# A staged kernel of attention and two expert layers: decode pieces of half the size, and one weight's loads issued earlier

## The chip, the cores and the metric

One core of a Trainium2 chip runs the whole program. The metric is the device time of one execution in microseconds; three runs of the kernel before gave 1173.73, 1179.30 and 1179.88, median 1179.3.

## The reference, cut to what matters

```python
def _attn_ref(q, k, v):                       # batch 4, 8 heads, 1152 positions, 64 wide
    q_pool = q.reshape(B, H, S // 2, 2, D).mean(axis=3)
    attn = softmax(scale * q_pool @ k.T)      # 576 queries against 1152 keys
    return attn @ v

def _moe_ref(x, w_in, w_out):                 # 2304 x 512 -> 2048 -> 512
    h = x @ w_in
    g = np.where(h >= 1, h, np.where(h <= -1, 0.0, (h + 1) ** 2 / 4))
    return g @ w_out
# then 8 experts of 512 -> 1024 -> 512, one for each token
```

The first layer's weights, `w_in` and `w_out`, come as 64-bit floats, so they are read as pairs of 32-bit words and turned into float32 by integer operations.

## The kernel before, in words

Three stages follow each other: attention, the first layer (`Moe1`), the routed experts (`Moe2`). The program's order is written out by hand: each engine runs its instructions in the order of the source.

*Attention* works on 16 pairs of heads, 9 query tiles of 128 each: 144 steps `s` (`t = s % 9`, and 8 more steps that only finish). In a step TensorE writes the scores of one tile into PSUM (L232), VectorE reads them into `e` and takes the minimum (L236), TensorE transposes the exponentials of an earlier tile (L261), ScalarE and VectorE split these into a high and a low part (L270, L272), and TensorE does eight matmuls of the product with `v` (L286). There is one PSUM buffer for scores, so the scores of step s + 1 wait for L236 of step s. GpSimd prepares the next pair, in the order of the steps: sum and split of q (L165, L57, L168, L169), split of k (L57, L174) and of v (L57, L195). SP issues nearly all DMAs.

At the end of each step `aside(s)` is called. From step 72 on it brings in the first three weights (`EARLY = 3`), 18 steps each: `ws.load(j)` issues two DMAs of 512 KB (a 128-wide slice of `w_in`, one of `w_out`), and `ws.decode(j)` gives six pieces for VectorE, three for each half: mask and shift (L458), a mask and or (L462), a shift and or (L466). After each third piece GpSimd copies the high part (L57) and subtracts (L451). The loads of weight 3 are issued at step 146 (`last` is 135).

`stage` is a pool of two large tiles (tag `m`) and two small ones (tag `w`); loads, decoded words and, at the end of attention, the rows of x for group 0 take turns in it. `tail()` at step 135 issues the DMAs of those rows; from step 139 on one x item a step is multiplied on GpSimd (L549, L550) and split by ScalarE and VectorE (L553, L554).

*Moe1* runs 16 steps of 128 hidden columns for each of four groups of tokens. `h_mm` writes h into one of two PSUM buffers (L577); `h_act` computes the activation: ScalarE (L592, L595), VectorE's product (L596), ScalarE's copy (L598), and the low part on GpSimd (L600). `fill()` puts one more decode piece into VectorE's queue, ahead of L596 and behind it; in group 0 five pieces a step decode weights 3 to 15, and the load of each half of the next weight follows the third and the sixth piece.

Of the kernel before, what the change touches and what calls it, by code (L numbers as in the profile page):

```python
# [8 lines left out]
F32 = mybir.dt.float32  # L9
F32R = mybir.dt.float32r  # L10
BF16 = mybir.dt.bfloat16
U32 = mybir.dt.uint32
I32 = mybir.dt.int32
AF = mybir.ActivationFunctionType
ALU = mybir.AluOpType
# [31 lines left out]
EARLY = 3  # L47
# [7 lines left out]
def hi_part(e, out, in_, nc):  # L55
    if e is nc.gpsimd:
        e.tensor_scalar(out=out, in0=in_, scalar1=1.0, scalar2=1.0, op0=ALU.mult, op1=ALU.mult)  # L57
    elif e is nc.scalar:
        e.copy(out, in_)
    else:  # L60
        e.tensor_copy(out, in_)
# [336 lines left out]
class Weights:  # L398
# [41 lines left out]
    def decode(self, j):  # L440


        nc = self.nc
        raw = self.raw
        hi, lo = (self.pools(j).tile([128, 2, 512], F32R, name=f"w{c}{j}", tag=f"w{c}{j}") for c in "hl")
        self.t[j] = hi, lo
        out = []

        def split(i, w, e):
            hi_part(e, hi[:, i], w, nc)  # L450
            nc.gpsimd.tensor_sub(out=lo[:, i], in0=w, in1=hi[:, i].bitcast(F32))  # L451

        for i in range(2):
            box = {}

            def first(i=i, box=box):
                box["w"] = self.stage.tile([128, 512], U32, name="wf", tag="w")
                nc.vector.tensor_scalar(out=box["w"], in0=raw[j, i][:, :, 1], scalar1=0x07FFFFFF, scalar2=3,  # L458
                                        op0=ALU.bitwise_and, op1=ALU.logical_shift_left)

            def second(i=i, box=box):
                nc.vector.scalar_tensor_tensor(out=box["w"], in0=raw[j, i][:, :, 1], scalar=0xC0000000,  # L462
                                               in1=box["w"], op0=ALU.bitwise_and, op1=ALU.bitwise_or)

            def third(i=i, box=box):
                nc.vector.scalar_tensor_tensor(out=box["w"], in0=raw[j, i][:, :, 0], scalar=29, in1=box["w"],  # L466
                                               op0=ALU.logical_shift_right, op1=ALU.bitwise_or)
                if j < EARLY:
                    split(i, box["w"].bitcast(F32), nc.gpsimd)
                else:  # L470
                    self.late.append(lambda: split(i, box["w"].bitcast(F32), nc.scalar))

            out += [first, second, third]
        return out
# [651 lines left out]
class Moe2:  # L1126
# [57 lines left out]
    def split(self, which, i):  # L1184
        k, h = divmod(i, 2)
        r, hi, lo = (self.w[which + c, k][:, h] for c in "rhl")
        self.nc.scalar.copy(hi, r)  # L1187
        self.nc.vector.tensor_sub(out=lo, in0=r, in1=hi.bitcast(F32))  # L1188
# [212 lines left out]
def tile_kernel(tc, q, k, v, w_in, w_out, emb, tau, w1, w2, out):  # L1401
    nc = tc.nc
    with ExitStack() as ctx:
        def pool(name, bufs, **kw):
            return ctx.enter_context(tc.tile_pool(name=name, bufs=bufs, **kw))

        one = pool("one", 1)
        dram = pool("dram", 1, space=DRAM)
        wa = pool("w_a", 1)
        stage = pool("stage", 2)  # L1410
        ctx.enter_context(tc.manual_schedule())

        idf = one.tile([128, 128], F32, name="idf")
        half = one.tile([128, 1], F32, name="half")
        zero = one.tile([128, 64], F32, name="zero")
        eps = one.tile([128, 1], F32, name="eps")
        cn = dict(idf=idf, half=half, zero=zero, eps=eps)
        xs = Scratch(dram)

        late = {}  # L1420
        ws = Weights(nc, w_in, w_out, stage, lambda j: wa if j < EARLY else late["w"])
        m1 = Moe1(tc, xs, ws, cn)
        with ExitStack() as actx:
            at = Attention(tc, q, k, v, xs, cn)
            make_identity(nc, idf)
            nc.vector.memset(half, 0.5)
            nc.vector.memset(eps, 1e-9)
            nc.vector.memset(zero, 0.0)
            at.open(actx)
            for w in range(2):  # L1430
                nc.scalar.copy(at.qts[0][:, w, NQ:NQ + 64], zero)
            for h in range(2):
                at.load_qk(0, h)
            rt = Router(tc, one, dram, emb, tau, cn)
            last = (at.NPAIR - 1) * 9
            pieces = []

            def aside(s):
                if s == 12:
                    late["consts"] = rt.consts(stage)  # L1440
                if 12 <= s < 12 + 3 * 6 and s % 3 == 0:
                    next(late["consts"], None)
                if s == 28:
                    late["emb"] = rt.experts(stage)
                if s in (31, 34):
                    late["emb"][(s - 31) // 3]()
                j, c = divmod(s - (last - 63), 18)
                if 0 <= j < EARLY:
                    if c == 0:
                        ws.load(j)  # L1450
                    elif c == 2:
                        pieces.extend(ws.decode(j))
                if pieces and s % 3 == 0:
                    pieces.pop(0)()
                if s == last + 11:
                    ws.load(EARLY)

            def tail():
                late["x0"] = tc.alloc_tile_pool(name="x0", bufs=1, side="right", reuse_waits="tile")
                m1.x_alloc(0, late["x0"])  # L1460

                for i in range(5):
                    m1.x_raw(0, i)
                    m1.x_load(0, i, ws.rows(i, 5))
                evs = {}

                def one(i):
                    evs[i] = m1.x_item(0, i)
                return [[lambda i=i: one(i) if i < 5 else None, lambda i=i: evs[i - 1]() if i else None]
                        for i in range(6)]  # L1470

            at.run(aside, tail)
        late["w"] = pool("w_b", 1, reuse_waits="tile")

        def weight(i, dt):
            j, c = divmod(i, 2)
            return ws.pools(j).tile([128, 2, 512], dt, name=f"e{i}", tag="w" + "hl"[c] + str(j))

        def xpool():
            late["x0"].release()  # L1480
            late["d_x"] = tc.alloc_tile_pool(name="d_x", bufs=1, side="right", reuse_waits="tile")
            return late["d_x"]

        rt.rtp, rt.rsm = pool("b_rt", 2, reuse_waits="tile"), pool("b_rs", 2, reuse_waits="tile")
        m2 = Moe2(tc, rt, w1, w2, out, weight, xpool, cn)
        with ExitStack() as bctx:
            x1 = bctx.enter_context(tc.tile_pool(name="x1", bufs=1, reuse_waits="tile"))
            m1.open(bctx)
            items = m1.run(rt, [late["x0"], x1], m2)
        with ExitStack() as dctx:  # L1490
            m2.open(dctx)
            m2.run(items)
        late["d_x"].release()
# [39 lines left out]
```

## Time and profile before

| what | us |
|---|---|
| median of three runs | 1179.3 |
| the profiled execution | 1178.18 |
| its span, first to last instruction | 1176.4 |
| TensorE matmul busy | 1135.4 (97%) |
| VectorE busy | 883.1 (75%) |
| ScalarE busy | 753.2 (64%) |
| GpSimd busy | 580.7 (49%) |

Attention takes the first 483 us of the span. A timeline row gives an instruction's start and length in us, engine, line, operation and operands, and in brackets the idle time of its engine just before it and what ended that. PE is TensorE, DVE VectorE, ACT ScalarE, POOL GpSimd, SPq the queue of SP. Ends of matmuls are modelled.

### The profile page before, as it was taken

The page shows a single profiled execution, that of the slowest core. Times are in us where ns is not written, and L with a number is a line of the kernel's source. Part 1 is how long each engine was busy: PE and PEld are TensorE (multiplying, and loading weights), DVE is VectorE, ACT ScalarE, POOL GpSimd, SP SyncE. Part 2 cuts the span into 40 slices and gives each one's busy share as a digit, 9 for nine tenths or more (in the row PEclk, how much of TensorE's full clock was granted, in tenths as well). Part 3 has the DMA queues.
Part 4 walks back from the last instruction along what each step waited for, and adds up shares of the span by engine and source line. Part 5 has one row for each costly group of instructions (what it writes and reads, how often), then busy time and mean ns, then how long its engine had stood idle before and what let it go on. Part 6 is the DMA issues. An engine that isn't in the chain of part 4 may idle for free. (4 is left out here: it accounts for less than half of the span.)

```text
span 1176.4 us, 21181 instructions
## 1 busy us (share of the span) xinstructions
PE 1135.4 (97%) x7315; PEld 1056.2 (90%) x7315; DVE 883.1 (75%) x1593; ACT 753.2 (64%) x1477; POOL 580.7 (49%) x499
## 2 busy tenths in 40 slices
PE   7999999999999999799999999999999999999997
PEld 6999999999999999799789999998889899887886
DVE  6898898899999998698866664764355776676765
ACT  5888888887878787555554445544435566566764
POOL 6998988887888885267762121112010221121212
PEclk9999999999999999899999999999999999999999
DMA  7777777786868758354532222120222121286443
GB/s 181 175 186 180 175 168 175 172 212 134 207 163 204 168 139 177 101 170 152 161 113 67 59 69 73 41 68 20 90 82 100 45 64 38 80 271 208 158 140 122
DMA packets 87877, 156.14 MB, mean 133 GB/s; under 512 B 26535, under 2 KB 44967, under 8 KB 87744
## 3 DMA queue, kind: packets, MB, share of 16 engines
q1 hardware_dynamic: 83040, 142.34, 45.4%
q0 software_dynamic: 4336, 11.58, 3.0%
q8 instruction: 67, 1.10, 0.4%
q10 hardware_dynamic: 368, 0.59, 0.2%
q14 instruction: 66, 0.54, 0.2%
HBM read 145.84 MB, written 20.08 MB: 141 GB/s over the span
## 5 line engine op out<-in xcount | busy, mean ns | idle before, releaser
L236 DVE TENSOR_SCALAR_CACHE_REDUCE e<-sc 128x1152 f32<-128x1152 f32 x144 | 194.7, 1352 | 24.3 <-PE sc L232 23.0
L243 ACT ACTIVATE e<-e,nm 128x1152 f32<-128x1152 f32 x144 | 183.6, 1275 | 9.0 <-DVE e L236 8.9
L232 PE MATMUL sc<-kT,qt 128*128 128x384 f32 x780 | 160.1, 340 | 11.7 <-DVE e L236 9.6
L270 ACT CAST pth<-pa 128x768 fp32r<-128x768 f32 (+2 forms) x160 | 116.3, 737 | 78.6 <-PE pa L261 78.4
L272 DVE TENSOR_TENSOR ptl<-pa,pth 128x768 fp32r<-128x768 f32 (+2 forms) x160 | 138.8, 876 | 17.7 <-ACT pth L270 5.5
L1188 DVE TENSOR_TENSOR e<-e,e 128x512 fp32r<-128x512 f32 x200 | 129.5, 688 | 28.3 <-ACT e L1187 12.3
L232 PEld LDWEIGHTS sc<-kT,qt 128*128 128x128 f32 x780 | 132.8, 189 | 14.5 <-DVE e L236 11.7
L596 DVE SCALAR_TENSOR_TENSOR u<-h,u 128x320 f32<-128x320 f32 (+1 forms) x112 | 55.7, 497 | 107.8 <-ACT u L595 107.4
L592 ACT ACTIVATE u<-h,half 128x320 f32<-128x320 f32 (+1 forms) x112 | 59.7, 533 | 109.5 <-PE h L577 109.3
L1284 PE MATMUL d_po<-e,e 128*128 128x512 f32 x504 | 121.0, 393 | 0.6 <-DVE e L1188 0.6
L261 PE MATMUL pa<-idf,e 128*128 128x128 f32 x864 | 117.6, 272 | 3.0 <-DVE ptl L272 3.0
L1187 ACT CAST e<-e 128x512 fp32r<-128x512 f32 x200 | 113.7, 619 | 0.6 <-issue 0.3
L609 PE MATMUL y<-wh,gh 128*128 128x512 f32 x288 | 113.9, 395 | 0.0
L609 PE MATMUL y<-wh,gl 128*128 128x512 f32 x288 | 113.7, 395 | 0.0
L609 PE MATMUL y<-wl,gh 128*128 128x512 f32 x288 | 113.6, 394 | 0.0
L261 PEld LDWEIGHTS pa<-idf,e 128*128 128x128 f32 x864 | 102.9, 140 | 8.3 <-issue 2.2
L1284 PEld LDWEIGHTS d_po<-e,e 128*128 128x128 f32 x504 | 92.6, 188 | 19.2 <-DVE e L1188 1.0
L1292 POOL DMA_INDIRECT out<-d_ob,d_rec x19 | 22.5, 1186 | 176.0 <-ACT d_ob L1291 119.3
L598 ACT CAST gh<-u 128x320 fp32r<-128x320 f32 (+1 forms) x112 | 52.3, 467 | 79.9 <-DVE u L596 79.9
L286 PE MATMUL av<-pth,vh 128*128 128x288 f32 x576 | 103.1, 306 | 0.0
L286 PE MATMUL av<-ptl,vh 128*128 128x288 f32 x576 | 102.2, 304 | 0.0
L577 PE MATMUL h<-xth,wh 128*128 128x320 f32 (+1 forms) x448 | 87.8, 318 | 8.3 <-DVE u L596 6.8
(258 smaller groups left out, 2533.8 us busy)
## 6 DMA issues: line engine op xcount, KB each, us to landing
e<-moe_w SPq DMA_DIRECT2D x104, 512.0 KB
kr<-k SPq DMA_DIRECT2D x63, 288.0 KB
qr<-q SPq DMA_DIRECT2D x62, 288.0 KB
kk<-kT SPq DMA_DIRECT2D x60, 288.0 KB
vr<-v SPq DMA_DIRECT2D x16, 576.0 KB
av_b<-avs SPq DMA_DIRECT2D x64, 128.0 KB
wi<-moe_w_in SPq DMA_DIRECT2D x16, 512.0 KB
wo<-moe_w_out SPq DMA_DIRECT2D x16, 512.0 KB
```

What stands on the lines that cost most here:

```text
L232: nc.tensor.matmul(s[:, j, 0:384], lhsT=a, rhs=b[:, 384 * j:384 * j + 384], start=i == 0, stop=i == len(mm) - 1)
L236: nc.vector.tensor_scalar(out=e.rearrange("p (a b) -> p a b", a=3), in0=s[:, :, 0:384], scalar1=-0.5 / D ** 0.5, scalar2=None, op0=ALU.mul ...
L243: self.nc.scalar.activation(e, e, AF.Exp, bias=d["nm"][:, t:t + 1], scale=-1.0, accum_out=d["sum"][:, t:t + 1])
L261: nc.tensor.transpose(p[:, c // 3, (c % 3) * 128:(c % 3) * 128 + 128], e[:, i * 128:(i + 1) * 128], idf)
L270: nc.scalar.copy(hi, p)
L272: nc.vector.tensor_sub(out=lo, in0=p, in1=hi.bitcast(F32))
L286: nc.tensor.matmul(box["t"][:, 0:GQ], lhsT=self.vh[:, h * 9 + i % 9], rhs=p[:, i % 9, c0:c0 + GQ], start=i == 0, stop=i == 17)
L577: nc.tensor.matmul(ps[:, :n], lhsT=a[:, k], rhs=b[:, k, h0:h0 + n], start=i == 0, stop=i == 11)
L609: self.nc.tensor.matmul(y, lhsT=a, rhs=b, start=j == 0 and q == 0, stop=j == NF - 1 and q == 2)
L1187: self.nc.scalar.copy(hi, r)
L1188: self.nc.vector.tensor_sub(out=lo, in0=r, in1=hi.bitcast(F32))
L1284: self.nc.tensor.matmul(self.o, lhsT=(self.hh, self.hl)[a][f // 4][:, f % 4, s], rhs=self.w[b, f // 2][:, f % 2], start=f == 0 and q == 0, ...
```

## The change

Two things. The pieces of the three weights decoded beside attention are cut in two by columns (256 instead of 512), twelve pieces a weight instead of six; one is put in at each step that is not a multiple of three, instead of at each that is. GpSimd's copy and subtraction are cut in the same way. Weights 3 to 15 keep pieces of 512 columns. And the two loads of weight 3 are issued at steps 142 and 144 (`last + 7`, `last + 9`) instead of both at 146.

```diff
+        early = j < EARLY
+        cols = (slice(0, 256), slice(256, 512)) if early else (slice(0, 512),)
+        box = {}
+        for i, c in ((i, c) for i in range(2) for c in cols):
 
-            def first(i=i, box=box):
-                box["w"] = self.stage.tile([128, 512], U32, name="wf", tag="w")
-                nc.vector.tensor_scalar(out=box["w"], in0=raw[j, i][:, :, 1], scalar1=0x07FFFFFF, scalar2=3,
+            def first(i=i, c=c):
+                if c.start == 0:
+                    box[i] = self.stage.tile([128, 512], U32, name="wf", tag="w")
+                nc.vector.tensor_scalar(out=box[i][:, c], in0=raw[j, i][:, c, 1], scalar1=0x07FFFFFF, scalar2=3,
                                         op0=ALU.bitwise_and, op1=ALU.logical_shift_left)
...
-                if j < EARLY:
-                    split(i, box["w"].bitcast(F32), nc.gpsimd)
+                if early:
+                    split(i, c, w.bitcast(F32), nc.gpsimd)
...
-                if pieces and s % 3 == 0:
+                if pieces and s % 3:
                     pieces.pop(0)()
-                if s == last + 11:
-                    ws.load(EARLY)
+                if s in (last + 7, last + 9):
+                    ws.load(EARLY, (s - last - 7) // 2)
```

## Rows read from the trace of the kernel before

**Rows 1.** Stretch table: bounds, length, busy us (instructions) of PE, PEld, DVE, ACT, POOL; PEclk, DMA share, GB/s.

```profile
245.00:425.00 180.00, 176.25 (x1300) 173.72 (x1299) 170.21 (x268) 144.59 (x266) 152.90 (x123) 1.00 0.74 180
...
492.10:495.40 3.30, 3.30 (x12) 3.30 (x13) 3.23 (x5) 2.31 (x5) 1.51 (x2) 0.50 0.09 23
```

**Rows 2.** Waits of TensorE (us, times, longest): 236 to 450, then whole span.

```profile
PE sc L232 <- DVE e L236: 3.8, 3, 1.7
...
PE h L577 <- DVE u L596: 6.8, 3, 5.1
```

**Rows 3.** Timeline of TensorE, attention: scores of four steps.

```profile
259.30 1.21 PE L232 MATMUL sc<-kT,qt 128*128 128x384 f32 x6
...
262.40 1.21 PE L232 MATMUL sc<-kT,qt 128*128 128x384 f32 x6
...
267.37 1.31 PE L232 MATMUL sc<-kT,qt 128*128 128x384 f32 x6 [1.72 <-DVE e L236]
...
325.43 1.31 PE L232 MATMUL sc<-kT,qt 128*128 128x384 f32 x6 [1.02 <-DVE e L236]
```

**Rows 4.** Timeline of VectorE, attention: reads of the scores and decode pieces.

```profile
250.75 1.36 DVE L236 TENSOR_SCALAR_CACHE_REDUCE e<-sc 128x1152 f32<-128x1152 f32 x1 [0.18 <-PE sc L232]
...
253.58 0.94 DVE L458 TENSOR_SCALAR wf<-wi 128x512 uint32<-128x512 uint32 x1
...
263.38 2.66 DVE L462 SCALAR_TENSOR_TENSOR wf<-wi,wf 128x512 uint32<-128x512 uint32 x1
...
309.49 1.36 DVE L236 TENSOR_SCALAR_CACHE_REDUCE e<-sc 128x1152 f32<-128x1152 f32 x1 [0.18 <-PE sc L232]
...
322.31 1.79 DVE L462 SCALAR_TENSOR_TENSOR wf<-wi,wf 128x512 uint32<-128x512 uint32 x1
```

**Rows 5.** Timeline of GpSimd, attention: preparation of the next pair, one weight split.

```profile
250.05 2.66 POOL L174 TENSOR_TENSOR kT<-kr,kT 64x1152 fp32r<-64x1152 f32 x1
252.79 1.44 POOL L165 TENSOR_TENSOR qr<-qr 128x576 f32<-128x576 f32 x1
...
262.83 2.67 POOL L174 TENSOR_TENSOR kT<-kr,kT 64x1152 fp32r<-64x1152 f32 x1
...
362.55 1.30 POOL L451 TENSOR_TENSOR wl<-wf,wh 128x512 fp32r<-128x512 f32 x1
...
366.72 1.42 POOL L168 TENSOR_TENSOR qt<-qr,qt 64x576 fp32r<-64x576 f32 x1
...
370.85 2.72 POOL L174 TENSOR_TENSOR kT<-kr,kT 64x1152 fp32r<-64x1152 f32 x1
373.65 1.43 POOL L165 TENSOR_TENSOR qr<-qr 128x576 f32<-128x576 f32 x1
```

**Rows 6.** Timeline of SP's queue, end of attention: the load of weight 3.

```profile
486.54 0.55 SPq L418 DMA_DIRECT2D wi<-moe_w_in  x1
```

**Rows 7.** Timeline of VectorE, start of the first layer.

```profile
491.21 0.43 DVE L458 TENSOR_SCALAR wf<-wi 128x512 uint32<-128x512 uint32 x1 [8.62 <-DMA wi<-moe_w_in]
...
511.32 0.49 DVE L596 SCALAR_TENSOR_TENSOR u<-h,u 128x320 f32<-128x320 f32 x1 [1.39 <-ACT u L595]
```

**Rows 8.** Timeline of ScalarE, start of the first layer.

```profile
485.84 0.47 ACT L595 ACTIVATE u<-u 128x320 f32<-128x320 f32 x1
```

**Rows 9.** Timeline of TensorE, start of the first layer.

```profile
492.09 1.43 PE L577 MATMUL h<-xth,wh 128*128 128x320 f32 x4 [5.09 <-DVE u L596]
```

**Rows 10.** Timeline of SP's queue, attention: loads of weights 0 and 1, a store.

```profile
241.85 0.59 SPq L418 DMA_DIRECT2D wi<-moe_w_in  x1
...
304.93 0.59 SPq L418 DMA_DIRECT2D wi<-moe_w_in  x1
...
311.51 0.45 SPq L318 DMA_DIRECT2D av_b<-avs  x1
```

**Rows 11.** Waits of SP's queue, 300 to 318 (us, times, longest).

```profile
SPq L318 <- DMA wi<-moe_w_in: 0.9, 1, 0.9
```

More of the change, by code (lines that the diff above doesn't have):

```diff
@@ L447, in decode, with split @@
         out = []
[L449 to L454, printed above, removed]
-            def first(i=i, box=box):
-                box["w"] = self.stage.tile([128, 512], U32, name="wf", tag="w")
-                nc.vector.tensor_scalar(out=box["w"], in0=raw[j, i][:, :, 1], scalar1=0x07FFFFFF, scalar2=3,
-                                        op0=ALU.bitwise_and, op1=ALU.logical_shift_left)
[L461 to L466, printed above, removed]
+        def split(i, c, w, e):
+            hi_part(e, hi[:, i, c], w, nc)
+            nc.gpsimd.tensor_sub(out=lo[:, i, c], in0=w, in1=hi[:, i, c].bitcast(F32))
@@ new lines, in decode, with second, third @@
+        early = j < EARLY
[6 more added lines that the diff above has]
+                nc.vector.tensor_scalar(out=box[i][:, c], in0=raw[j, i][:, c, 1], scalar1=0x07FFFFFF, scalar2=3,
+                                        op0=ALU.bitwise_and, op1=ALU.logical_shift_left)
+            def second(i=i, c=c):
+                w = box[i][:, c]
+                nc.vector.scalar_tensor_tensor(out=w, in0=raw[j, i][:, c, 1], scalar=0xC0000000,
+                                               in1=w, op0=ALU.bitwise_and, op1=ALU.bitwise_or)
+            def third(i=i, c=c):
+                w = box[i][:, c]
+                nc.vector.scalar_tensor_tensor(out=w, in0=raw[j, i][:, c, 0], scalar=29, in1=w,
@@ L467, in third @@
                                                op0=ALU.logical_shift_right, op1=ALU.bitwise_or)
-                if j < EARLY:
-                    split(i, box["w"].bitcast(F32), nc.gpsimd)
+                if early:
+                    split(i, c, w.bitcast(F32), nc.gpsimd)
                 else:
-                    self.late.append(lambda: split(i, box["w"].bitcast(F32), nc.scalar))
+                    self.late.append(lambda: split(i, c, w.bitcast(F32), nc.scalar))
             out += [first, second, third]
```

## The prediction

> **What bounds the kernel now.** I read first the stretch table, then TensorE's waits, then the timelines of single engines around those waits. In the stretch of attention that holds the decoding, TensorE is busy 176.25 of 180 us, but VectorE is close behind with 170.21 and GpSimd works 152.90 [rows 1]. TensorE sets the time; VectorE has about 0.3 us to spare in a step. The reader is to see two places where TensorE waits for something that the change touches [rows 2]: 3.8 us in three waits inside the decode stretch, all for VectorE's read of the scores, and, of 6.8 us for VectorE in the first layer, one wait of 5.1.
>
> The first place. An attention step takes 3.10 us (262.40 - 259.30) [rows 3]. The next scores can only be written when VectorE has read the last ones, and a decode piece sits in VectorE's queue just ahead of that read. Two pieces show the price: one of 2.66 us [rows 4] makes TensorE wait 1.72, one of 1.79 makes it wait 1.02 [rows 3]. So a piece costs its length less 0.77 to 0.94; I use **0.85 free per step**. The long pieces are not long by their work. The 2.66 us one began at 263.38, inside a GpSimd subtraction that ran from 262.83 to 265.50, and ended 0.54 after it [rows 4, 5]. The first kind of piece (a mask and shift, with one tensor input) is held as well: at 253.58 it took 0.94 and ended 0.29 after the GpSimd addition that began at 252.79 [rows 4, 5]. So a piece that meets a two-input GpSimd operation waits for its end, and then needs about 0.55 (0.29 for the first kind).
>
> Here a rule of the Trainium skill speaks against the change. The page "SBUF — State Buffer", section "Who interferes with whom", says that VectorE and GpSimd share a port pair as an exclusive lock, held for a whole instruction, and that "Issue order, not op shape, decides who blocks." These rows agree, and by the rule the sum is the one below. If a stall shrank with the piece instead, the decode stretch would simply give back its 3.8 us.
>
> The second place. The loads of weight 3 stand in SP's queue behind the last pair's sums and the first of its stores, and go out at 486.54 [rows 6]. VectorE idles 8.62 us for them and starts the first piece at 491.21 [rows 7]. That piece stands ahead of the product that frees a PSUM buffer, whose ScalarE input was there at 486.31 [rows 8]. TensorE loses 5.09 us [rows 9], and in the 3.30 us after it the granted clock is 0.50, the lower of its two levels (1.2 GHz), with TensorE busy throughout [rows 1].
>
> **Part 1: the load is issued at steps 142 and 144 instead of 146.** Two DMAs of 512 KB move, no bytes are added. They pass one queue, SP's, and in it the four DMAs of the last pair's sums and the first four of its stores. A wait is added there: each load needs a staging tile that the x items of group 0 hold until VectorE's subtraction of item 1 (or 3), some steps before attention ends. Behind the waiting load on SP stand only those sums and stores, which can't go before VectorE has finished attention, so nobody is hurt. With 4.7 us from issue (486.54) to use (491.21) the weights are there before 486.31, and the first piece runs in VectorE's idle time. Gains:
> - the wait: 5.09, since the product can then run at 486.31 and TensorE is busy until about then;
> - the clock: half of 3.30, 1.65, if no gap of this length is left;
> - what is late next: the second and third piece stand ahead of the second half's product. Their lengths lie between 0.4 and 1.8 us (a blocked one, [rows 4]); TensorE without its gap and its low clock reaches that product some 1.65 us earlier against VectorE. I take 0.5 us off, between 0 and 1.8.
> Given back later? TensorE would run 1.1 us further ahead of the decoding than now. At 511.32 VectorE still waits 1.39 us for ScalarE's, and so TensorE's, result [rows 7], so this lead is absorbed there. Sum: 5.09 + 1.65 - 0.5 = **6.2 us gained**, between 3.3 and 6.7.
>
> **Part 2: the three weights decoded beside attention go in halves.** 18 pieces become 36, in two of every three steps instead of one; each third piece is followed on GpSimd by half a copy and half a subtraction, 12 pairs instead of 6. Nothing leaves VectorE but the fixed part of an instruction is paid 18 times more. Unblocked, a half piece is below 0.55 plus a start, so about 0.4, under the 0.85 that a step has free: this costs nothing, and is covered only as long as GpSimd does not hold it. What is removed is at most the 3.8 us [rows 2]. What is added I work out by where the new steps fall in GpSimd's round, which repeats with every pair (9 steps, t = 0 to 8; the old pieces sat at t = 0, 3, 6, the new ones at 1, 2, 4, 5, 7, 8).
> - **The very first one** (step 74). VectorE became free there at 250.57 (its next read started at 250.75 after 0.18 idle [rows 4]), and its weight, sent for at 241.85 [rows 10], is there by the landing time below (6.6 us). GpSimd's long subtraction began at 250.05 and ran 2.66 us, to 252.71 [rows 5]. Up to this point nothing differs from before, so the piece waits 2.14 and needs 0.15: 2.3 - 0.85 = 1.5 us lost.
> - **t = 7, from the GpSimd chain.** A third piece at t = 5 releases the half copy and half subtraction. The full subtraction takes 1.30 [rows 5]; I put the half at 0.7 and the copy, a one-input operation, at 0.4, estimates, with 0.25 for the gaps. Then come the operations of the t = 6 to 8 rows: the long subtraction starts 4.13 us after the first of them (370.85 - 366.72), the next addition 6.93 after (373.65) [rows 5]. So the long one starts 5.5 us after the third piece ended. The piece of t = 7 comes two steps after that of t = 5 began, so 6.2 - 0.4 = 5.8 after its end, 0.3 us inside the long subtraction, with 2.4 to wait: 1.6 lost. For weight 0 I count this.
> - **In the later five pairs** the third piece at t = 5 is itself likely held by a few tenths, which moves the chain behind it; then the piece of t = 7 slips in ahead of the long subtraction, and that of t = 8 (8.9 after) meets the addition that starts at 8.3. Two shorter holds of about 1.0 to 1.4, each with some lateness carried over, cost 0.5 to 0.6 each: 1.1 a pair. If the chain is not moved it is 1.6 plus 0.5. The ends are 0.3 and 2.4; I take 1.1, the row-by-row order above being the nearest: 5 x 1.1 = 5.5.
> - **The weight is not there yet** (steps 92 and 110). Weights 1 and 2 are loaded at steps 90 and 108 as before, but the first piece now comes one step earlier. For weight 1 SP issued the load at 304.93, and at 311.51 it went on with a store [rows 10] which had waited for that load [rows 11]: it lands at about 311.5, 6.6 us later, in a stretch whose DMA engines are 74% busy [rows 1]. VectorE is free for the piece at 309.31 (309.49 - 0.18, [rows 4]): 2.2 us of waiting, 0.3 for the piece, and on average 0.6 for a GpSimd operation met on the way (0 to 1.4). Behind it on VectorE stands the read of the scores, and behind that TensorE. (The second half of each load now waits on SP for a piece that ends at step 91 or 109 instead of 90 or 108; behind it stand the sums and stores of the pair before, which wait for VectorE there anyway, and no one waits for those: nothing.) 3.1 - 0.85 = 2.2, twice: 4.4, between 3.2 and 6.
> Sum of part 2: 1.5 + 1.6 + 5.5 + 4.4 - 3.8 = **9.2 us lost**. Low end: 1.5 + 0 + 1.5 + 3.2 - 3.8 = 2.4. High end: 1.5 + 1.6 + 12 + 6 - 3.8 = 17.3.
>
> **The sum.** 9.2 - 6.2 = +3.0. The profiled execution took 1178.18 us (span 1176.4 and 1.8 around it), so 1181.2 by its own time; the median of the runs is 1.1 above it, and I forecast 1182.3 for a median. The runs before spread over 6 us, so about 0.5% (5.9 us) is what can be told from no change.
>
> **The rivals.**
> - *The halves fit.* If half pieces were held no more than the tolerance, the decode stretch would give back up to 3.8 and the change would gain 6.2 + 3.8 = 10 us: 1169. For it: the holds from the chain have margins of 0.3 us, which can fall the other way. Against it: the first hold follows from unchanged rows, and so does the load that lands late. With only these two kept (1.5 + 3.2) it is 1179.3 + 4.7 - 3.8 - 6.2 = 1174. Chance 0.2 for a time below 1177, of which 0.13 are beyond 0.5%.
> - *GpSimd's lock takes over* (the other side). One mechanism, at t = 7: if the chain after t = 5 is not moved, every pair's first piece falls into the 2.7 us subtraction. It decides from the point where the subtraction starts before the piece, a margin of 0.3 us. Price 2.1 to 2.4 for each of five pairs instead of 1.1, and the late loads at 2.6 each: 1182.3 + 5 x 1.1 + 0.8 = 1189. Chance 0.25.
> - *The earlier load gains little.* If a load sat behind something on SP, or VectorE's decoding became the bound in group 0, only part 1's low end would remain: 1185. For it: TensorE waits again for decoded weights late in group 0; against it: the 1.39 us of slack at 511.32. Chance 0.08.
> - *The forecast*, between 1177 and 1186: the remaining 0.47.
>
> **How the numbers follow.** Faster by over 0.5% needs part 2 to cost almost nothing: 0.13. Slower by over 0.5% comes from the lock rival and the upper end of the forecast: 0.25. Within 0.5%: 0.62. The range goes from the middle of the first rival, 1173.5, to the lock rival, 1189.5.
>
> **What would show it.** Part 1: no wait of TensorE near 487, no low clock after it, the weight's loads issued before the last sums, and VectorE's first piece right behind the transposed sums. Part 2: TensorE's waits for VectorE's read of the scores rise from 3.8 to 10 to 17 us in the decode stretch; half pieces of 2 us and more beside GpSimd's long subtraction at step 74 and at t = 7; about 2 us of VectorE waiting for the DMA at the first pieces of weights 1 and 2. I am wrong if half pieces stay near 0.4 us throughout, or if the weights land before 309.

## The result and the profile after

The changed kernel takes 1189.99 us (median of 5 runs, 1186.94 to 1191.95), against 1179.12 for the kernel before (1173.73 to 1179.88). The ratio is 1.0088, with a 95% interval of 1.0066 to 1.0110: slower, by some 10.4 us (7.8 to 13.0). The forecast was 1182.3, with a range of 1173.5 to 1189.5. So the sign of the forecast was right, the loss was some 7.5 us larger than forecast, and the median lies half a microsecond past the upper end. The likeliest case, a time within 0.5% of before (chance 0.62), did not come; the slower one (0.25) did.

The head of the page of the changed kernel, the profiled execution of 1188.15 us:

```profile
span 1186.3 us, 21183 instructions
...
PE 1144.8 (96%) x7315; PEld 1061.5 (89%) x7315; DVE 893.5 (75%) x1611; ACT 754.5 (64%) x1477; POOL 579.3 (49%) x511
```

The span is 9.9 us longer than before's 1176.4. Three marks in the timelines of both kernels show where: the first `h` matmul of the first layer, ScalarE's first copy of `y` into `rows` (the end of group 0's hidden columns), and the same copy for group 2.

| from | to | before, us | after, us | difference |
|---|---|---|---|---|
| start | first `h` matmul | 483.32 | 496.82 | +13.5 |
| first `h` matmul | first copy, group 0 | 127.25 | 121.71 | -5.5 |
| group 0 | group 2 | 223.67 | 223.66 | 0.0 |
| group 2 | end | 342.2 | 344.1 | +1.9 |

The first row is part 2 (the half pieces), and 0.5 us the other way in the first 20 us, where TensorE's clock came up a little sooner than in the execution of before (granted 1.00 between 15 and 20 us, against 0.71). The second row is part 1 (the earlier load). The last row has unchanged code; over the eight kernels of this study it lies between 342.2 and 345.5, so it is read as variation.

**Part 1 in the profile.** SP's queue at the end of attention: the first half of weight 3 goes out at 482.86, the second at 491.11, both ahead of the last pair's sums (L310).

```profile
481.86 0.60 SPq L319 DMA_DIRECT2D av_t<-avs  x1
482.86 0.40 SPq L418 DMA_DIRECT2D wi<-moe_w_in  x1
491.11 0.37 SPq L423 DMA_DIRECT2D wo<-moe_w_out  x1
496.12 1.36 SPq L310 DMA_DIRECT2D rs_b<-rt  x4
```

VectorE's first piece of weight 3 then waits for no DMA (before: 8.62 us, [rows 7]), and it is VectorE that waits at the product, for ScalarE:

```profile
496.01 0.39 DVE L461 TENSOR_SCALAR wf<-wi 128x512 uint32<-128x512 uint32 x1
499.84 0.49 DVE L601 SCALAR_TENSOR_TENSOR u<-h,u 128x320 f32<-128x320 f32 x1 [3.44 <-ACT u L600]
```

On TensorE the wait of 5.09 us [rows 9] has shrunk to 0.37, at the first layer's second half, and the granted clock in the stretch that begins with the first `h` matmul is 1.00, where it was 0.50 behind the old wait [rows 1]:

```profile
502.78 0.85 PE L582 MATMUL h<-xth,wh 128*128 128x320 f32 x4 [0.37 <-DVE u L601]
```

```profile
496.80:506.00 9.20, 8.83 (x56) 8.19 (x55) 6.06 (x7) 4.64 (x10) 3.45 (x3) 1.00 0.49 129
```

**Part 2 in the profile.** The waits in 236 to 450 (us, times, longest); TensorE's for the read of the scores were 3.8 us in three [rows 2]:

```profile
PE sc L232 <- DVE e L236: 6.8, 10, 1.4
...
PE sc L232 <- POOL qr L165: 5.4, 3, 1.8
DVE wf L461 <- DMA wi<-moe_w_in: 1.8, 2, 1.0
```

The second line names GpSimd, but the wait is VectorE's. Here are the scores of steps 76, 78 and 81 on TensorE, then VectorE's pieces and its read of the scores, then GpSimd, all of the first decoded pair:

```profile
253.67 1.83 PE L232 MATMUL sc<-kk,bd 128*128 128x384 f32 x9 [1.45 <-DVE e L236]
...
261.41 1.32 PE L232 MATMUL sc<-kT,qt 128*128 128x384 f32 x6 [0.77 <-DVE e L236]
...
272.77 1.44 PE L232 MATMUL sc<-kT,qt 128*128 128x384 f32 x6 [1.82 <-POOL qr L165]
```

```profile
249.95 2.39 DVE L461 TENSOR_SCALAR wf<-wi 128x256 uint32<-128x256 uint32 x1
...
258.56 1.52 DVE L466 SCALAR_TENSOR_TENSOR wf<-wi,wf 128x256 uint32<-128x256 uint32 x1
...
262.61 0.41 DVE L471 SCALAR_TENSOR_TENSOR wf<-wi,wf 128x256 uint32<-128x256 uint32 x1
...
268.68 2.67 DVE L461 TENSOR_SCALAR wf<-wi 128x256 uint32<-128x256 uint32 x1
271.27 1.34 DVE L236 TENSOR_SCALAR_CACHE_REDUCE e<-sc 128x1152 f32<-128x1152 f32 x1
...
301.49 0.28 DVE L461 TENSOR_SCALAR wf<-wo 128x256 uint32<-128x256 uint32 x1
...
315.96 0.84 DVE L461 TENSOR_SCALAR wf<-wi 128x256 uint32<-128x256 uint32 x1 [1.01 <-DMA wi<-moe_w_in]
```

```profile
249.52 2.67 POOL L174 TENSOR_TENSOR kT<-kr,kT 64x1152 fp32r<-64x1152 f32 x1
...
258.38 1.42 POOL L195 TENSOR_TENSOR vh<-vr,vh 128x576 fp32r<-128x576 f32 x1
...
268.54 2.66 POOL L174 TENSOR_TENSOR kT<-kr,kT 64x1152 fp32r<-64x1152 f32 x1
271.28 1.40 POOL L165 TENSOR_TENSOR qr<-qr 128x576 f32<-128x576 f32 x1
...
301.48 2.82 POOL L174 TENSOR_TENSOR kT<-kr,kT 64x1152 fp32r<-64x1152 f32 x1
```

The reader is to see three held pieces. The piece at 249.95 ends 0.15 us after the subtraction of 249.52; the one at 258.56 ends 0.28 after the subtraction of v (L195); the one at 268.68, whose own work is 0.28 us (its like at 301.49), began 0.14 us after L174 and ran 2.67, to 0.15 past its end. VectorE's read of the scores follows and ends at 272.61, and the scores of step 81 start at 272.77. GpSimd's L165, which has nothing to do with these scores, ended at 272.68, so the wait bears its name. At 301.49 VectorE and L174 started within 0.01 us of each other; there the piece ran free, and the subtraction took 2.82 instead of 2.66.

The copies of GpSimd, with one input, hold a piece too. Here two copies of q lie beside a second piece, VectorE's row first:

```profile
322.83 0.90 DVE L466 SCALAR_TENSOR_TENSOR wf<-wi,wf 128x256 uint32<-128x256 uint32 x1
```

```profile
322.15 1.31 POOL L57 TENSOR_SCALAR qt<-qr 128x576 fp32r<-128x576 f32 x2
```

The piece ends 0.27 us after the copies, much as the one beside L195 did; where nothing holds it, it takes 0.41 (at 273.88).

For each pair of heads I add up how much later than its regular distance every score begins: 3.10 us from the last one, and 3.62 where the step before has t = 4 with its nine matmuls. The timeline of TensorE gives the starts. The waits view shows less, 12.2 us for after, since the ends of matmuls are modelled, so that each wait is understated by some 0.15, and since a low clock and small lateness are no waits to it.

| kernel | 74 to 82 | 83 to 91 | 92 to 100 | 101 to 109 | 110 to 118 | 119 to 127 | 128 to 136 | sum |
|---|---|---|---|---|---|---|---|---|
| before | 2.0 | 0.1 | 1.3 | 0.0 | 0.0 | 1.3 | 0.0 | 4.6 |
| after | 6.4 | 1.5 | 3.8 | 1.5 | 3.8 | 1.5 | 0.2 | 18.6 |
| part 1 alone | 2.0 | 0.0 | 1.3 | 0.0 | 0.1 | 1.3 | 0.0 | 4.7 |
| part 2 alone | 4.8 | 1.5 | 5.4 | 2.9 | 1.5 | 1.6 | 0.2 | 17.9 |
| whole, moved | 1.2 | 0.1 | 0.0 | 0.0 | 0.0 | 0.0 | 0.0 | 1.3 |
| halves, moved | 1.0 | 1.6 | 1.5 | 1.5 | 1.6 | 1.5 | 0.7 | 9.4 |
| subtraction in two | 2.3 | 1.8 | 2.3 | 1.7 | 2.2 | 1.8 | 0.2 | 12.2 |
| load sooner | 4.8 | 1.5 | 1.6 | 1.6 | 1.6 | 1.6 | 0.2 | 12.9 |

So part 2 lost 18.6 - 4.6 = 14.0 us in the traces and part 1 gave 5.5 back.

### The profile page after: what moved, and what is told of

It is laid out like the page before. It is cut to its first block, busy times and chain, and to the rows that moved or that the text cites. A ratio compares the mean times of both kernels' runs of the same rounds, so it can differ in the third digit from the quotient of the medians.

```text
span 1186.3 us, 21183 instructions
## 1 busy us (share of the span) xinstructions
PE 1144.8 (96%) x7315; PEld 1061.5 (89%) x7315; DVE 893.5 (75%) x1611; ACT 754.5 (64%) x1477; POOL 579.3 (49%) x511
```

## The experiments

Theory: VectorE's pieces are held by whole GpSimd operations, and TensorE pays for what a step can't absorb. Rivals: the number of instructions on VectorE is what costs; the weights' landing is what costs; or part 1 brings less than it seems and part 2 more.

**Part 1 alone**, in the kernel before:

```diff
-                if s == last + 11:
-                    ws.load(EARLY)
+                if s in (last + 7, last + 9):
+                    ws.load(EARLY, (s - last - 7) // 2)
```

> Part 1 alone: whole pieces at every third step as before, the loads of weight 3 at steps 142 and 144. Lock theory: part 1 gains what the changed kernel showed between the last attention step and the first rows of group 0, 5.5 us, so about 1173.6; no wait of 5 us for VectorE in the first layer and no low clock behind it; the decode stretch keeps its 3.8 us of waits. Rival (the early load gains little, decoding bounds group 0 anyway): 1177 or more, with the gain given back before 610 us.

Measured: 1173.77 us (1170.52 to 1175.60), ratio 0.9936 (0.9913 to 0.9959), which is 7.5 us faster (4.8 to 10.3). In the trace the stretch from the first `h` matmul to group 0's first copy is 122.94, 4.3 less than before, and the decode stretch is unchanged (4.7 against 4.6). The forecast of 6.2 lies between the two. A part of the lead is given back here: at 564.05 TensorE waits 2.14 us for VectorE's product (1.43 at the same place in before), and the granted clock is 0.57 from 564 to 568. The whole profiled execution is only 2.9 us shorter than before's (spans of 1173.5 and 1176.4), mainly because a low clock at the end of attention cost it another 1.6 us (last section). This is the fastest kernel of the study together with "whole, moved" below, and it beats both the kernel before and the changed one.

**Part 2 alone**: the changed kernel with the load of weight 3 back at step 146.

```diff
-                if s in (last + 7, last + 9):
-                    ws.load(EARLY, (s - last - 7) // 2)
+                if s == last + 11:
+                    ws.load(EARLY)
```

> Part 2 alone: half pieces as in the changed kernel, the loads of weight 3 at step 146 as before. Lock theory: 14 us slower than the kernel before, about 1193, with the long holds at step 74 and at t = 7 of every second pair, and the wait of 5 us in the first layer back. Rival (part of the loss came with the early load): 1186 to 1190.

Measured: 1196.25 us (1190.85 to 1198.32), ratio 1.0127 (1.0100 to 1.0153), which is 15.0 us slower (11.8 to 18.0). The trace loses 17.9 - 4.6 = 13.3 in the decode stretch, and the stretch behind the first `h` matmul is 127.06, as in before (127.25). So the two parts act apart: +15.0 and -7.5 make +7.5, and the whole change measured +10.4, within what these intervals allow. Part 2 was mis-sized, not part 1.

The decode code is that of the changed kernel, yet the holds fall otherwise. The first half of weight 2 (110 to 118) has neither a hold at t = 7 nor a wait for the DMA, and the second half of weight 1 (101 to 109) has a long hold at t = 7, although its third piece was held as well (1.06 us at 356.40). VectorE, then GpSimd:

```profile
362.99 2.79 DVE L461 TENSOR_SCALAR wf<-wo 128x256 uint32<-128x256 uint32 x1
```

```profile
362.97 2.65 POOL L174 TENSOR_TENSOR kT<-kr,kT 64x1152 fp32r<-64x1152 f32 x1
```

The piece began 0.02 us after L174 and was held; one pair of weight 0 has the same 0.02 us (299.33 and 299.31), and there the piece took 0.28 and ran free. At such margins the recorded starts do not tell which engine waits. The long holds do not stand in every second pair, as had been expected.

**Whole pieces at steps that meet GpSimd less**: part 1, with pieces of 512 columns at t = 0, 3, 5.

```diff
-                if pieces and s % 3 == 0:
+                if pieces and s % 9 in (0, 3, 5):
```

> Part 1, and whole pieces at t = 0, 3, 5 of each pair instead of 0, 3, 6; their size and number are those of before. Lock theory: the piece that met GpSimd's subtractions at t = 6 now meets none, the decode stretch loses 0 to 1.5 us instead of 4.4, so 3 to 4.4 us below part 1 alone, about 1169.5. Rival (what a piece costs depends on its size and number, not on where it falls): the same as part 1 alone, about 1173.6.

Measured: 1174.00 us (1172.31 to 1178.51), ratio 0.9947 (0.9927 to 0.9967). In the trace one wait is left of three:

```profile
PE sc L232 <- DVE e L236: 1.0, 1, 1.0
```

The decode stretch loses 1.3 instead of 4.7, and the second piece, which took 2.66 us in before [rows 4], is held by a subtraction of q (L169) in the first pair and takes 1.90; in the later pairs it starts just ahead of the subtraction of v (L195) and takes 0.68. GpSimd's row is the last:

```profile
259.18 1.90 DVE L462 SCALAR_TENSOR_TENSOR wf<-wi,wf 128x512 uint32<-128x512 uint32 x1
...
288.77 0.68 DVE L462 SCALAR_TENSOR_TENSOR wf<-wo,wf 128x512 uint32<-128x512 uint32 x1
```

```profile
259.13 1.41 POOL L169 TENSOR_TENSOR qt<-qr,qt 64x576 fp32r<-64x576 f32 x1
```

Where nothing holds it, a whole piece needs 0.68 us, less than the 0.85 that a step has free. What the place is worth, 3.4 us in the trace, does not come out of the timed runs: the ratio is not told apart from that of part 1 alone.

**Half pieces away from t = 7 and t = 2**: the changed kernel with the pieces at t = 0, 1, 3, 4, 5, 6, as many as before per pair.

```diff
-                if pieces and s % 3:
+                if pieces and s % 9 in (0, 1, 3, 4, 5, 6):
```

> The changed kernel with its half pieces at t = 0, 1, 3, 4, 5, 6 instead of 1, 2, 4, 5, 7, 8; size and number stay. Lock theory: no half meets the long subtraction except now and then, the weights have landed when the first pieces come, the decode stretch loses 2 to 4 us instead of 18: about 1175. Rival (36 small pieces are too many for a VectorE that is 95% busy, wherever they stand): 1187 to 1190.

Measured: 1180.46 us (1174.19 to 1183.63), ratio 0.9999 (0.9981 to 1.0017). The place of the pieces alone is worth 9.5 us against the changed kernel's median, with the same number of instructions. That speaks against the rival of the count. But the loss in the trace is 9.4 us and not the 2 to 4 that I had set: the long holds are gone, and every pair keeps some 1.5 us in small ones. VectorE and GpSimd at the second of them:

```profile
287.18 0.98 DVE L466 SCALAR_TENSOR_TENSOR wf<-wo,wf 128x256 uint32<-128x256 uint32 x1
...
290.70 1.06 DVE L471 SCALAR_TENSOR_TENSOR wf<-wo,wf 128x256 uint32<-128x256 uint32 x1
```

```profile
286.46 1.43 POOL L165 TENSOR_TENSOR qr<-qr 128x576 f32<-128x576 f32 x1
...
290.06 1.43 POOL L195 TENSOR_TENSOR vh<-vr,vh 128x576 fp32r<-128x576 f32 x1
```

Six pieces a pair instead of three stand in GpSimd's round, and in each pair behind the first three of them are held and take 0.8 to 1.2 us. Each of these two, whose own work is about 0.4, takes 1.0 and makes the scores 0.2 and 0.5 us late.

**GpSimd's long subtraction in two**: the changed kernel with L174 as two instructions of half the columns, same work.

```diff
-            return [lambda: hi_part(f, kt[:, h], kr, nc),
-                    lambda: e.tensor_sub(out=kt[lo, h], in0=kr[lo], in1=kt[lo, h].bitcast(F32))]
+            def sub():
+                for c in ((slice(0, S),) if n == 0 else (slice(0, S // 2), slice(S // 2, S))):
+                    e.tensor_sub(out=kt[lo, h, c], in0=kr[lo, c], in1=kt[lo, h, c].bitcast(F32))
+            return [lambda: hi_part(f, kt[:, h], kr, nc), sub]
```

> The changed kernel, with GpSimd's long subtraction (L174, 64x1152) made in two halves by columns; VectorE's work is untouched. Lock theory: a piece that meets it is held at most 1.4 us instead of 2.7, so the three or four waits of TensorE of 1.6 to 2.0 us shrink to 0.2 to 0.7 each: 5 to 7 us below the changed kernel, about 1184. Rival (VectorE's own load sets the loss, or GpSimd's total work): no change, or slower by the extra GpSimd instructions, 1190 or more.

Measured: 1182.87 us (1179.01 to 1184.61), ratio 1.0024 (1.0010 to 1.0038): 7 us better than the changed kernel, by an edit that touches no decode piece. In the trace it is 6.4, of which 1.7 are the first pair's low clock; the four delays of 1.6 to 2.0 us behind L174 are now 0.4 to 0.7. The two pieces that took 2.39 and 2.67 are now held for the rest of one half only:

```profile
249.65 1.15 DVE L463 TENSOR_SCALAR wf<-wi 128x256 uint32<-128x256 uint32 x1
...
267.14 1.43 DVE L463 TENSOR_SCALAR wf<-wi 128x256 uint32<-128x256 uint32 x1
```

This shows directly that the length of the GpSimd instruction sets the length of the hold. The prediction had put the Trainium skill's rule ("SBUF — State Buffer", "Who interferes with whom") beside its rows, a lock held for a whole instruction; this run agrees with it. The rows at 301.48 and 301.49 show that GpSimd can be the one to lose (0.16 us there), but at 0.01 to 0.02 us apart the recorded starts do not say which engine came first.

**The weights sooner**: the changed kernel with each half of weights 1 and 2 loaded earlier.

```diff
-                    if c == 0:
-                        ws.load(j)
+                    if c == 0 and j == 0:
+                        ws.load(0)
                     elif c == 2:
+                        if j:
+                            ws.load(j, 1)
                         pieces.extend(ws.decode(j))
+                    elif c == 16 and j + 1 < EARLY:
+                        ws.load(j + 1, 0)
```

> The changed kernel, with the first halves of weights 1 and 2 loaded two steps sooner (steps 88 and 106) and the second halves at 92 and 110. Lock theory with the late landing: VectorE's wait for the DMA goes, and with it TensorE's two waits of 1.34 us; the two pairs behind it then run as the pairs with the second halves do (1.3 us lost instead of 3.4): 3 to 4.5 us below the changed kernel, about 1186. Rival (the wait for the DMA was slack of VectorE): at most 1 us.

Measured: 1183.18 us (1180.70 to 1190.39), ratio 1.0039 (1.0023 to 1.0056). The waits for the DMA are gone, and the pairs of the first halves of weights 1 and 2 lose 1.6 us instead of 3.8. Without its first pair's low clock the changed kernel loses 4.0 us more than this one in the trace, as had been expected; by the timed ratios the two are 5.8 apart. The 2.2 us of a pair are more than the 1.34 us that TensorE lost at step 94 for the late landing: the hold at t = 7 went as well. VectorE in this kernel, and GpSimd:

```profile
322.86 1.06 DVE L471 SCALAR_TENSOR_TENSOR wf<-wi,wf 128x256 uint32<-128x256 uint32 x1
...
329.45 0.28 DVE L461 TENSOR_SCALAR wf<-wi 128x256 uint32<-128x256 uint32 x1
```

```profile
329.46 2.80 POOL L174 TENSOR_TENSOR kT<-kr,kT 64x1152 fp32r<-64x1152 f32 x1
```

The third piece, at t = 5, is held here (1.06 us instead of the 0.41 at 326.26 in the changed kernel), so the copy and subtraction behind it, and with them L174, start later, and the piece of t = 7 slips in 0.01 us ahead. In the changed kernel the same piece began 0.16 us after L174 (332.36 against 332.20):

```profile
326.26 0.41 DVE L471 SCALAR_TENSOR_TENSOR wf<-wi,wf 128x256 uint32<-128x256 uint32 x1
...
332.36 2.64 DVE L461 TENSOR_SCALAR wf<-wi 128x256 uint32<-128x256 uint32 x1
```

```profile
332.20 2.65 POOL L174 TENSOR_TENSOR kT<-kr,kT 64x1152 fp32r<-64x1152 f32 x1
```

## Why the prediction was right or wrong, step by step

- **Part 1, 6.2 gained: right.** 5.5 in the trace of the changed kernel, 4.3 to 6.2 over the six kernels that have the early load, 7.5 (4.8 to 10.3) timed alone. The wait fell from 5.09 to 0.37 and the low clock behind it is gone. The term "what is late next", 0.5, was of the right kind: VectorE's queue at the second half's product, 0.37. What is given back later was put at nothing; in the changed kernel two later waits for VectorE's product in group 0 come to 2.03 us where they were 1.66, with part 1 alone to some 3.4.
- **Part 2, 9.2 lost: right mechanism, too small.** It was 14.0 in the trace, inside the part's own ends of 2.4 and 17.3.
- *The very first piece*, 1.5: right, 1.6.
- *t = 7 of weight 0*, 1.6: right, 1.97. The subtraction started 5.5 us after the third piece's end (263.02 to 268.54), as worked out, and the piece came 0.14 us into it. The margin of 0.3 was smaller than the working could decide, so that it fell this way is in part luck.
- *The second piece of weight 0*: missed, 0.94. I went through GpSimd's long subtraction and its addition and never put the subtraction of v at t = 5 (L195) beside the piece of step 76. The row at 258.56 shows it, and the halves moved have the same hold at the same place.
- *The low clock of the first pair*: missed, 1.69 (below).
- *The later five pairs*, 1.1 each: the order of events was right and is what three of them did, at 1.5 (two holds that cost 0.5 and 0.7, and some 0.1 more in each of several steps). The holds had the forecast length, 1.06 and 1.30 us, but only 0.57 and 0.60 of it were free there, not 0.85; each stood behind a step with a piece of its own, and whether that is the reason is not shown. In the two pairs of a `w_in` half the third piece was not held, and there the rival of GpSimd's lock came true: 1.95 and 1.99 at t = 7, and some 0.5 around it. The prediction took one order for all five; it gave the margin as 0.3 us, and the trace of the changed kernel shows 0.11 to 0.16 one way and 0.01 or less the other. In part 2 alone, of the later pairs, one of each kind had the long hold.
- *The weight that is not there yet*, 2.2 twice: right in kind, 1.34 each. The load landed 6.6 us after its issue, as worked out (309.38 to 315.96 in the changed kernel), but VectorE came to it later than in before, because the step ahead had lost 0.7 us, and waited only 1.01. The second time it waited 0.78, and in part 2 alone there was no second wait.
- *What is removed*, 3.8: 4.6 by the starts of the scores.
- *VectorE's 0.3 us to spare in a step*: misread. [rows 1] leave 9.79 us idle in some 56 steps, under 0.2 a step; no term of the sum used it.

By pairs: 3.1 forecast and 6.4 measured for the first, 3.3 and 4.5 for the three of `w_out` halves, 6.6 and 7.6 for the two of `w_in` halves, 0 and 0.2 behind them, less 3.8 and 4.6. The largest miss is the first pair, 3.3 us: a hold not looked for and a clock that fell. The last stage's 1.9 us in the profiled execution have no cause in the change that I can show, nor is it settled how much of the timed 10.4 they make.

The range ended at the lock rival, 1189.5, which priced five pairs at 2.2. What came was that rival in two of the five pairs, and with it two terms that the sum had not. Pairs that can fall on either side of a margin of 0.1 to 0.3 us should have been taken as five separate throws, and the range's upper end by the sum of the part's own high end, 17.3 - 6.2 = +11.1, or 1190.4.

## What to carry to other kernels

An instruction that waits for another engine's whole instruction does not get cheaper by being halved: the hold stays, and there are twice as many. Before cutting work into smaller pieces, lay each new place against every operation of the other engine, the short ones and the copies too. Two other levers gave time back against the changed kernel: moving the half pieces (9.5 us) and cutting the operation that holds them (7 us); neither ran faster than the kernel before. Moving whole pieces took 3.4 us out of the trace, but not out of the timed runs. A load that stands in a queue behind the end of a stage can be worth more than the work it feeds: two lines that send it earlier gave 0.6% here.

## What the runs showed of the hardware that I had not expected

TensorE's granted clock fell to the lower of its two levels after waits that were all short. In the changed kernel the waits of 1.45, 0.77 and 1.82 us above, within 20 us, were followed by this stretch:

```profile
268.00:273.00 5.00, 3.18 (x24) 2.95 (x23) 5.00 (x6) 2.69 (x6) 4.75 (x4) 1.00 0.42 89
273.00:278.00 5.00, 5.00 (x26) 4.90 (x26) 4.04 (x7) 3.54 (x7) 1.18 (x3) 0.66 0.88 210
```

"Load sooner" has the same three waits (1.6, 0.94 and 1.98 by the starts of the scores, as in the changed kernel) and kept its clock at 1.00 behind them; part 2 alone kept it there too and lost 1.67 us in the same way eighteen steps later. With part 1 alone the clock stood at 0.52 in the 3 us after three waits of 0.58, 0.95 and 1.94 at the end of attention, and in before, with 0.58, 0.95 and 1.96 at the same place, at 1.00:

```profile
476.00:479.00 3.00, 3.00 (x15) 3.00 (x15) 2.38 (x4) 2.30 (x5) 0.00 (x0) 0.52 0.45 135
```

```profile
476.00:479.00 3.00, 3.00 (x25) 3.00 (x26) 2.36 (x5) 2.99 (x8) 0.00 (x0) 1.00 0.02 5
```

This is not an effect of the early load: part 2 alone, whole moved and halves moved have the same loss at the end of attention (14.2 us from the last scores to the first `h` matmul), while the changed kernel, "subtraction in two" and "load sooner" have 12.65, as before has. So the same waits were followed by a fall in one execution and by none in another; what decides stays open. It is worth about 1.5 to 1.7 us each time.
